# Ordered first loads on one queue, and attention features made a tile ahead, in a cosFormer attention and FFN kernel

## The chip, the cores and the metric

The kernel runs on one core of one Trainium2 chip. The metric is the device time of one execution in microseconds (us). All stage times below count from the start of the profiled span, which is about 2 us shorter than the timed execution. PE is the matrix engine (PEld its weight loads), ACT ScalarE, DVE VectorE, POOL GpSimd, SP the sync engine.

## The reference, cut to what matters

```
# q, k, v: (batch 8, heads 8, sequence 576, head_dim 64), f32
phi(x) = concat(relu(x) * cos(theta_s), relu(x) * sin(theta_s))     # 128 features
kv  = sum_s phi(k)^T v ;  z = sum_s phi(k)
x   = phi(q) kv / (phi(q) z + 1e-6)            # -> 4608 tokens x 512
out = ((x @ w1) * (x @ w2)) @ w3 @ w_out       # w1, w2: 512x1024, w3: 1024x1024, w_out: 1024x512
```

Nothing is nonlinear between w3 and w_out, so the kernel multiplies these two once at the start (its `w34b`) and then needs three products per FFN tile of 512 tokens. There are eight batches of attention and nine FFN tiles.

## The kernel before

The weights come on POOL's queue, which casts them to bf16 on the way, and the first two batches on SP's queue beside them. The features of batch 0 stand between the two halves of the weight product:

```
for i in range(4):
    nc.gpsimd.dma_start(out=w3b[:, 0:4, ts(i, 256)], in_=w3v[:, 0:4, ts(i, 256)])
    nc.gpsimd.dma_start(out=woutb[:, ts(i, 2), :], in_=wov[:, ts(i, 2), :])
    ...
for i in range(2):
    nc.gpsimd.dma_start(out=w3b[:, 4:8, ts(i, 512)], in_=w3v[:, 4:8, ts(i, 512)])
cosv, sinv = _trig_tables(nc, const)
...
load(0)                                   # k, v, q on nc.sync, six transfers
for i in range(4):                        # w1 and w2 in quarters on nc.gpsimd
    ...
load(1)                                   # on nc.sync
...
w34_half(0)
for c in range(NCH):
    prep(0, c)                            # features of batch 0
w34_half(1)
for u in attention_units(0):
    u()
```

`prep(b, c)` makes the features of one of five sequence chunks with five instructions: a relu and scale of k and of q on DVE and again on ACT, and the copy of v into `va` on POOL. Attention of a batch is twenty units: five kv products, five transposes of q features, five num steps (a PE product, then three DVE instructions that divide by the denominator), and five transposes of the result into the FFN input. All num steps share one PSUM tile, so they form a serial chain through PE and DVE.

The FFN tile t is cut into 24 groups of four matmuls each. Between the groups stand the features and then the attention units of batch t+1, both in the same tile:

```
todo = pr[0:2] + [f for p in zip(pr[2:], at[0:3]) for f in p] + at[3:]
```

For odd batches the first q transpose in that list takes chunk 4, whose features were issued last.

## Time and profile before

| | before |
|---|---|
| time, median (range) | 308.52 us (308.38 to 308.71, 4 runs) |
| profiled span | 306.4 us |
| first FFN matmul of tile 0 | 55.3 |
| first FFN matmul of tile 1 | 91.9 |
| tiles 2 to 6 | 141.7 in all |
| tiles 7, 8 and tail | 45.4 |

The page's line of PE's busy time, and the PE clock that was granted in each fortieth of the span, in tenths of full speed:

```profile
PE 265.0 (86%) x2074; PEld 141.8 (46%) x2112; DVE 160.2 (52%) x358; ACT 141.5 (46%) x249; POOL 38.0 (12%) x68
PEclk9999599796899999999999999999999999999999
```

PE is busy for 86% of the span. Of the 41 us in which it is not, 30 lie in the first third (before 91.9): there it waits, and the clock falls to 0.5 to 0.8 in some slices. About 5 of the rest are waits in tiles 2, 4 and 6. Two lines of the timeline bound the serial chain of attention of batch 0 (start, duration, engine, line, operation):

```profile
46.19 0.43 DVE L202 CAST kvs<-pnum 128x260 bf16<-128x260 f32 x1
...
55.25 0.61 PE L278 MATMUL ffnps<-xT,w1b 128*128 128x512 bf16 x1
```

From the end of the kv copy (46.6) to the first FFN matmul it takes 8.6.

### The profile page before, as it was taken

How to read it: one execution, taken by the hardware profiler on the slowest of the kernel's cores; microseconds unless marked ns; L12 is line 12 of the kernel's file. 1: busy time of each engine (PE TensorE's matmuls, PEld its weight loads, DVE VectorE, ACT ScalarE, POOL GpSimd, SP SyncE). 2: the span in 40 equal slices, each digit the busy share in tenths (PEclk: the TensorE clock that was granted, in tenths of full speed). 3: DMA queues.
4: the chain of work that ended last, by engine and by line, in shares of the span. 5: the costliest groups of instructions: out<-in, count | busy, mean ns of one | idle time of the engine just before them, and what ended most of it. 6: DMA issues, size and time to landing. Idle time of an engine off the chain costs nothing.

```text
span 306.4 us, 5315 instructions
## 1 busy us (share of the span) xinstructions
PE 265.0 (86%) x2074; PEld 141.8 (46%) x2112; DVE 160.2 (52%) x358; ACT 141.5 (46%) x249; POOL 38.0 (12%) x68
## 2 busy tenths in 40 slices
PE   0176795895989999799999998999999799999994
PEld 0133364342655554455555544555554455444441
DVE  0425248373666665666568474848746485240420
ACT  1006532274249436823862593269247524433332
POOL 8322412040000300030003002100300000000000
PEclk9999599796899999999999999999999999999999
DMA  8999999970029914981594389039812002102103
GB/s 193 246 238 224 235 238 239 300 165 2 13 92 240 257 28 137 255 186 49 174 260 122 104 225 259 19 136 260 203 71 68 2 0 91 49 0 105 34 2 135
DMA packets 51385, 43.33 MB, mean 141 GB/s; under 512 B 13985, under 2 KB 46753, under 8 KB 51361
## 3 DMA queue, kind: packets, MB, share of 16 engines
q1 hardware_dynamic: 42880, 37.75, 46.6%
q0 software_dynamic: 8480, 5.24, 11.5%
q8 instruction: 16, 0.26, 0.4%
q14 instruction: 9, 0.07, 0.1%
HBM read 38.80 MB, written 9.44 MB: 157 GB/s over the span
## 4 chain that ended last, share of the span: by engine, by line
PE 77%; ACT 9%; DVE 6%; issue 4%; DMA 3%; POOL 0%; ACTq 0%; POOLq 0%
PE ffnps L292 20%; PE ffnps L278 18%; PE ffnps L285 17%; PE ffnps L133 6%; PE pst L210 6%; ACT qp L181 4%; PE pnum L218 4%; PE pnum L196 3%; ACT kp L177 3%; DMA woutb<-in_moe_w_out_dram 3%; PE pst L244 2%; ACT asb L281 2%; DVE xblk L225 1%; PE pst L140 1%; DVE kp L175 1%
## 5 line engine op out<-in xcount | busy, mean ns | idle before, releaser
L287 DVE TENSOR_TENSOR abT<-asb,ffnps 128x512 bf16<-128x512 bf16 x72 | 49.4, 686 | 61.1 <-PE ffnps L285 56.4
L285 PE MATMUL ffnps<-xT,w2b 128*128 128x512 bf16 x285 | 75.0, 385 | 0.3 <-issue 0.2
L278 PE MATMUL ffnps<-xT,w1b 128*128 128x512 bf16 x268 | 73.2, 386 | 2.0 <-issue 0.7
L292 PE MATMUL ffnps<-w34b,abT 128*128 128x512 bf16 x275 | 69.7, 379 | 0.7
L281 ACT CAST asb<-ffnps 128x512 bf16<-128x512 f32 x72 | 41.8, 581 | 60.3 <-PE ffnps L278 60.3
L178 POOL CAST va<-vs 128x512 bf16<-128x512 f32 (+1 forms) x40 | 23.3, 626 | 164.1 <-DMA vs<-in_v_dram 138.4
L285 PEld LDWEIGHTS <-w2b 128*128 128x128 bf16 x288 | 27.3, 100 | 28.8 <-issue 2.1
L278 PEld LDWEIGHTS <-w1b 128*128 128x128 bf16 x288 | 25.4, 99 | 25.2 <-issue 1.9
L245 ACT COPY xT<-pst 128x512 bf16<-128x512 bf16 (+1 forms) x40 | 21.7, 544 | 30.4 <-PE pst L244 30.4
L297 ACT COPY osb<-ffnps 128x512 f32<-128x512 f32 x36 | 21.1, 585 | 30.6 <-PE ffnps L292 30.6
L292 PEld LDWEIGHTS <-abT 128*128 128x128 bf16 x288 | 25.0, 98 | 21.3
L211 DVE COPY qpT<-pst 128x1024 bf16<-128x1024 bf16 (+1 forms) x40 | 25.3, 632 | 14.1 <-PE pst L210 13.8
L210 PE MATMUL pst<-identb,qp 128*128 128x128 bf16 (+1 forms) x320 | 23.4, 217 | 8.8 <-ACT qp L181 8.8
L133 PE MATMUL ffnps<-woutb,w3T 128*128 128x512 bf16 x62 | 19.8, 451 | 11.2 <-DVE w3T L145 11.2
L177 ACT ACTIVATE kp<-ks,sinv 128x512 bf16<-128x512 f32 (+1 forms) x40 | 28.9, 722 | 0.0
L181 ACT ACTIVATE qp<-qs,sinv 128x512 bf16<-128x512 f32 (+1 forms) x40 | 28.5, 712 | 0.0
L225 DVE TENSOR_TENSOR xblk<-pnum,den 128x512 bf16<-128x512 f32 (+1 forms) x40 | 27.6, 689 | 1.4
L210 PEld LDWEIGHTS <-qp 128*128 128x128 bf16 (+1 forms) x320 | 18.8, 99 | 16.6 <-ACT qp L181 10.8
L218 PEld LDWEIGHTS <-qpT 128*128 128x128 bf16 (+1 forms) x320 | 14.4, 100 | 15.5 <-DVE xblk L225 6.5
L222 DVE TENSOR_SCALAR den<-pnum 128x8 f32<-128x8 f32 (+1 forms) x40 | 6.5, 163 | 28.1 <-PE pnum L218 28.1
L218 PE MATMUL pnum<-kvs,qpT 128*128 128x65 bf16 (+1 forms) x320 | 17.0, 194 | 4.0 <-DVE xblk L225 2.9
L196 PEld LDWEIGHTS <-kp 128*128 128x128 bf16 (+1 forms) x320 | 15.1, 99 | 10.5 <-issue 4.1
(40 smaller groups left out, 149.2 us busy)
## 6 DMA issues: line engine op xcount, KB each, us to landing
ks<-in_k_dram SPq DMA_DIRECT2D x8, 1024.0 KB, 7.8
vs<-in_v_dram SPq DMA_DIRECT2D x8, 1024.0 KB, 11.5
qs<-in_q_dram SPq DMA_DIRECT2D x8, 1024.0 KB, 10.7
out_dram<-osb SPq DMA_DIRECT2D x32, 256.0 KB, 2.3
ks<-in_k_dram SPq DMA_DIRECT2D x8, 128.0 KB, 8.2
w3b<-in_moe_w_dram POOLq DMA_DIRECT2D x4, 256.0 KB, 11.4
woutb<-in_moe_w_out_dram POOLq DMA_DIRECT2D x4, 256.0 KB, 12.7
vs<-in_v_dram SPq DMA_DIRECT2D x8, 128.0 KB, 11.5
```

The lines of the kernel that those rows point to most:

```text
L133: nc.tensor.matmul(acc[jp][:, :], lhsT=w3T[:, ts(jp, 128)], rhs=woutb[:, lc, :], start=(lc == 0), stop=(lc == 7))
L177: nc.scalar.activation(out=kp[:R, c, :, D:F], in_=ks, func=ACTF.Relu, scale=sc, bias=0.0)
L181: nc.scalar.activation(out=qp[:R, c, :, D:F], in_=qs, func=ACTF.Relu, scale=sc, bias=0.0)
L210: nc.tensor.transpose(pst[:, h, 0:R], qp[:R, c, h, :], identb[:R, :R])
L211: nc.vector.tensor_copy(out=att[b]["qpT"][:, :, ds(128 * c, R)], in_=pst[:, :, 0:R])
L218: nc.tensor.matmul(nt[:R, h // 4, ds((h % 4) * 65, 65)], lhsT=qpT[:, h, ds(128 * c, R)], rhs=kvs[:, h, :], start=True, stop=True)
L225: nc.vector.tensor_tensor(out=xblk[:R], in0=n4[:, :, :, 0:D], in1=den[:R].unsqueeze(3).to_broadcast([R, 2, 4, D]), op=ALU.mult)
L278: nc.tensor.matmul(aT[:, :], lhsT=w1b[:, kc, ts(jc, 128)], rhs=x[:, kc, :], start=(kc == 0), stop=(kc == 3))
L281: nc.scalar.copy(out=asb[:], in_=aT[:, :])
L285: nc.tensor.matmul(bT[:, :], lhsT=w2b[:, kc, ts(jc, 128)], rhs=x[:, kc, :], start=(kc == 0), stop=(kc == 3))
L287: nc.vector.tensor_mul(out=abT[:, jc, :], in0=asb[:], in1=bT[:, :])
L292: nc.tensor.matmul(ops[:, :], lhsT=abT[:, jc, ts(ms, 128)], rhs=w34b[:, jc, :], start=(jc == 0), stop=(jc == 7))
```

## The change

Its intent is twofold. The first loads all go on POOL in the order of their use, so that the weight product no longer shares the transfer engines with batches 0 and 1; the features of batch 0 move behind the whole weight product. And the features of batch t+2 are made in tile t, so that in tile t the attention of batch t+1 never waits for features just issued. In tile 0 this leaves features of batch 1 in the last nine groups and puts the whole attention of batch 1 behind the tile.

```diff
+    cosv, sinv = _trig_tables(nc, const)
     identb = const.tile([P, P], BF16, name="identb")
-    for i in range(4):
-        nc.gpsimd.dma_start(out=w3b[:, 0:4, ts(i, 256)], in_=w3v[:, 0:4, ts(i, 256)])
-        nc.gpsimd.dma_start(out=woutb[:, ts(i, 2), :], in_=wov[:, ts(i, 2), :])
+    for i, (c0, n) in enumerate(((0, 2), (2, 2), (4, 4))):
+        ls = slice(128 * c0, 128 * (c0 + n))
+        nc.gpsimd.dma_start(out=w3b[:, 0:4, ls], in_=w3v[:, 0:4, ls])
+        nc.gpsimd.dma_start(out=woutb[:, c0:c0 + n, :], in_=wov[:, c0:c0 + n, :])
 ...
-    load(0)
-    for i in range(4):
-        cs = ts(i, 256)
-        nc.gpsimd.dma_start(out=w1b[:, :, cs], in_=w1v[:, :, cs])
-        nc.gpsimd.dma_start(out=w2b[:, :, cs], in_=w2v[:, :, cs])
-    load(1)
+    load(0, nc.gpsimd)
+    for c0, n in ((0, 256), (256, 256), (512, 512)):
+        nc.gpsimd.dma_start(out=w1b[:, :, ds(c0, n)], in_=w1v[:, :, ds(c0, n)])
+        nc.gpsimd.dma_start(out=w2b[:, :, ds(c0, n)], in_=w2v[:, :, ds(c0, n)])
+    load(1, nc.gpsimd)
 ...   (prep is split into prep_k: k features and the v copy, and prep_q)
     w34_half(0)
-    for c in range(NCH):
-        prep(0, c)
     w34_half(1)
-    for u in attention_units(0):
+    for u in prep_units(0) + attention_units(0):
         u()
 ...
+        if t == 0:
+            spread(prep_units(1), 15, 23, slots)
+            slots[23] += prep_units(2)[0:4] + attention_units(1) + prep_units(2)[4:]
+            load(2, nc.sync)
+        else:
+            if t + 2 < B:
+                spread(prep_units(t + 2), 0, 22, slots)
+                if t + 3 < B:
+                    load(t + 3, nc.sync)
+            if t + 1 < B:
+                spread(attention_units(t + 1), 0, 22, slots)
 ...   (behind the groups of the tile)
+        if t == 0:
+            load(3, nc.sync)
```

More of the change, by code (lines that the diff above doesn't have):

```diff
@@ L98 @@
     for i in range(2):
-        nc.gpsimd.dma_start(out=w3b[:, 4:8, ts(i, 512)], in_=w3v[:, 4:8, ts(i, 512)])
-    cosv, sinv = _trig_tables(nc, const)
+        nc.gpsimd.dma_start(out=w3b[:, ds(4 + 2 * i, 2), :], in_=w3v[:, ds(4 + 2 * i, 2), :])
     va_bufs = []
@@ L108, with load @@
     raw = {}
-    def load(b):
+    def load(b, eng):
         got = []
@@ L113, in load @@
             t = ld.tile([P, H, 4, D], FP32, name=name + "s")
-            nc.sync.dma_start(out=t[:], in_=src[b, :, 0:512, :].rearrange("h (p j) d -> p h j d", j=4))
+            eng.dma_start(out=t[:], in_=src[b, :, 0:512, :].rearrange("h (p j) d -> p h j d", j=4))
             t4 = ld.tile([64, H, D], FP32, name=name + "s4")
-            nc.sync.dma_start(out=t4[:], in_=src[b, :, 512:S, :].rearrange("h p d -> p h d"))
+            eng.dma_start(out=t4[:], in_=src[b, :, 512:S, :].rearrange("h p d -> p h d"))
             got.append((t, t4))
         raw[b] = got
-    load(0)
-    for i in range(4):
-        cs = ts(i, 256)
-        nc.gpsimd.dma_start(out=w1b[:, :, cs], in_=w1v[:, :, cs])
-        nc.gpsimd.dma_start(out=w2b[:, :, cs], in_=w2v[:, :, cs])
-    load(1)
+    load(0, nc.gpsimd)
[3 more added lines that the diff above has]
+    load(1, nc.gpsimd)
     def w34_half(half):
@@ L158, with prep_k @@
     feat = {}
-    def prep(b, c):
+    def prep_k(b, c):
         R = ROWS[c]
@@ L169, in prep, with prep_q @@
         kp, qp, va = feat[b]
-        (k0, k4), (v0, v4), (q0, q4) = raw[b]
+        (k0, k4), (v0, v4), _ = raw[b]
         ks = k0[:, :, c, :] if c < 4 else k4[:]
         vs = v0[:, :, c, :] if c < 4 else v4[:]
-        qs = q0[:, :, c, :] if c < 4 else q4[:]
-        cc, sc = cosv[:R, c:c + 1], sinv[:R, c:c + 1]
-        nc.vector.tensor_scalar(out=kp[:R, c, :, 0:D], in0=ks, scalar1=0.0, scalar2=cc,
-                                op0=ALU.max, op1=ALU.mult)
-        nc.scalar.activation(out=kp[:R, c, :, D:F], in_=ks, func=ACTF.Relu, scale=sc, bias=0.0)
-        nc.gpsimd.tensor_copy(out=va[:R, c, :, 0:D], in_=vs)
-        nc.vector.tensor_scalar(out=qp[:R, c, :, 0:D], in0=qs, scalar1=0.0, scalar2=cc,
-                                op0=ALU.max, op1=ALU.mult)
-        nc.scalar.activation(out=qp[:R, c, :, D:F], in_=qs, func=ACTF.Relu, scale=sc, bias=0.0)
+        nc.vector.tensor_scalar(out=kp[:R, c, :, 0:D], in0=ks, scalar1=0.0,
+                                scalar2=cosv[:R, c:c + 1], op0=ALU.max, op1=ALU.mult)
+        nc.scalar.activation(out=kp[:R, c, :, D:F], in_=ks, func=ACTF.Relu,
+                             scale=sinv[:R, c:c + 1], bias=0.0)
+        nc.gpsimd.tensor_copy(out=va[:R, c, :, 0:D], in_=vs)
+    def prep_q(b, c):
+        R = ROWS[c]
+        qp = feat[b][1]
+        q0, q4 = raw[b][2]
+        qs = q0[:, :, c, :] if c < 4 else q4[:]
+        nc.vector.tensor_scalar(out=qp[:R, c, :, 0:D], in0=qs, scalar1=0.0,
+                                scalar2=cosv[:R, c:c + 1], op0=ALU.max, op1=ALU.mult)
+        nc.scalar.activation(out=qp[:R, c, :, D:F], in_=qs, func=ACTF.Relu,
+                             scale=sinv[:R, c:c + 1], bias=0.0)
     att = {}
@@ L300, in ffn_groups, with prep_units @@
             yield
+    def prep_units(b):
+        return ([(lambda c=c: prep_k(b, c)) for c in range(NCH)]
+                + [(lambda c=c: prep_q(b, c)) for c in range(NCH)])
     w34_half(0)
-    for c in range(NCH):
-        prep(0, c)
     w34_half(1)
@@ L308, with spread @@
     fsb = ctx.enter_context(tc.tile_pool(name="fsb", bufs=3))
-    for u in attention_units(0):
+    for u in prep_units(0) + attention_units(0):
         u()
+    def spread(units, first, last, slots):
+        for i, u in enumerate(units):
+            slots[min(last, first + int(i * (last + 1 - first) / len(units)))].append(u)
     for t in range(NT):
-        groups = ffn_groups(t)
-        n = 24
-        b = t + 1
-        todo = []
-        if b < B:
-            if b + 1 < B:
-                load(b + 1)
-            first = 8 if t == 0 else 0
-            pr = [(lambda c=c: prep(b, c)) for c in range(NCH)]
-            at = attention_units(b)
-            todo = pr[0:2] + [f for p in zip(pr[2:], at[0:3]) for f in p] + at[3:]
-            per = len(todo) / (n - first)
-        done = 0
-        for g in range(n):
-            next(groups)
-            if todo:
-                want = min(len(todo), int(round((g + 1 - first) * per)))
-                while done < want:
-                    todo[done]()
-                    done += 1
-        for _ in groups:
-            pass
-        while todo and done < len(todo):
-            todo[done]()
-            done += 1
+        slots = [[] for _ in range(24)]
+        if t == 0:
[9 more added lines that the diff above has]
+                spread(attention_units(t + 1), 0, 22, slots)
+        for g, _ in enumerate(ffn_groups(t)):
+            for u in slots[g]:
+                u()
+        if t == 0:
+            load(3, nc.sync)
 _INS = ['q', 'k', 'v', 'moe_w1', 'moe_w2', 'moe_w3', 'moe_w_out']
```

## The prediction

> **What bounds the kernel now.** I read the page by slices first, then the POOL instructions in order of time, the chain of waits by stage, and one table by stretches. Times are microseconds from the start of the span; the span is 306.4 and the timed run 308.48, so 2.1 lie outside.
>
> The slices (7.66 us each) show two stages:
>
> ```profile
> PE   0176795895989999799999998999999799999994
> DMA  8999999970029914981594389039812002102103
> GB/s 193 246 238 224 235 238 239 300 165 2 13 92 240 257 28 137 255 186 49 174 260 122 104 225 259 19 136 260 203 71 68 2 0 91 49 0 105 34 2 135
> ```
>
> For the first eight slices the transfer engines are full and PE is not. From slice 12 on PE is nearly full and the transfers have holes. So the start is set by the order in which bytes arrive, and the rest by PE. The stages in numbers, cut at the FFN tile starts in the chain that ended last:
>
> ```profile
> 0.00:56.08 56.08, 30.56 (x268) 17.72 (x271) 22.73 (x69) 17.21 (x29) 20.39 (x38) 0.93 1.18 236
> 91.89:119.33 27.44, 27.23 (x233) 14.87 (x237) 17.84 (x39) 15.42 (x28) 2.84 (x5) 1.00 0.65 168
> 119.33:148.38 29.05, 27.00 (x233) 14.91 (x238) 17.97 (x39) 15.62 (x29) 2.84 (x5) 1.00 0.63 159
> 148.38:175.60 27.22, 27.01 (x233) 14.72 (x236) 17.83 (x39) 15.84 (x29) 2.84 (x5) 1.00 0.66 170
> 175.60:204.69 29.09, 27.04 (x234) 14.96 (x238) 17.97 (x39) 15.67 (x29) 2.84 (x5) 1.00 0.61 159
> ```
>
> The second column is the length, the third the PE busy time. FFN tiles 1 and 3 take about 27.3 with 27.0 to 27.2 of PE; tiles 2 and 4 (and 6, 29.10) take 29.1 with the same PE work. The waits of PE name the difference: the first line is tile 0, the second a stretch of tiles 3 and 4.
>
> ```profile
> PE pst L210 <- ACT qp L181: 3.8, 1, 3.8
> PE pst L210 <- ACT qp L181: 1.7, 1, 1.7
> ```
>
> For an odd batch the attention takes chunk 4 first, so the transpose of its q feature stands right behind the ten feature instructions that ScalarE still works off. It occurs in tiles 0, 2, 4 and 6, whose next batch is odd.
>
> The POOL instructions show how the start is queued:
>
> ```profile
> 7.01 0.73 POOL L95 DMA_DIRECT2D woutb<-in_moe_w_out_dram  x1
> 8.40 0.77 POOL L99 DMA_DIRECT2D w3b<-in_moe_w_dram  x1 [0.65 <-DMA w3b<-in_moe_w_dram]
> 10.43 0.74 POOL L99 DMA_DIRECT2D w3b<-in_moe_w_dram  x1 [1.26 <-DMA woutb<-in_moe_w_out_dram]
> 13.58 0.76 POOL L123 DMA_DIRECT2D w1b<-in_moe_w_dram  x1 [1.78 <-DMA w3b<-in_moe_w_dram]
> 32.87 0.74 POOL L124 DMA_DIRECT2D w2b<-in_moe_w_dram  x1 [3.46 <-DMA w3b<-in_moe_w_dram]
> 33.60 2.83 POOL L178 CAST va<-vs 128x512 bf16<-128x512 f32 x5
> ```
>
> Eight transfers go out at once; the ninth waits for a w3b landing at 8.4, the tenth for a woutb, the eleventh for a w3b, and so on to the eighteenth. I read this as: **transfer n on this queue is issued when transfer n-8 has landed**. The copies of v for batch 0 stand behind the eighteenth. Today that costs nothing, because attention of batch 0 begins only at 43.1.
>
> **What the Trainium skill says.** "DMA: Bandwidth & Descriptors", section "Queues, rings and completion order": each transfer engine takes turns between the queues that have work, packet by packet. The trace agrees: the last eight weight pieces (4096 packets) land between 32.9 and 56.7 while the loads of q, k, v move 3.5 MB. The same page, "Issuing engines are not separate DMA queues": issuing from several engines only saves issue time. Here too the total stays near 236 GB/s with two queues, so one ordered queue loses nothing by itself; no stretch of this trace has the weight queue alone. "PSUM — Partial Sum Buffer", "Engine vs sequencer instructions": the queues of ScalarE, VectorE and GpSimd are strict FIFO. The va copies behind the last issue at 32.87 agree. "TensorE: Matmul & The Clock Gate", Part 1: an idle window halves the PE clock, some 3.4 us of work restore it. The trace agrees in kind: four 128x512 matmuls take 0.86 in the chain when warm, so eight take 1.73; after attention of batch 0, in which PE is idle for half of the time, the first eight of tile 0 take from 55.32 to 58.58, or 3.26. I charge 1.5 for such a start.
>
> **The change part by part.** *(a) Order of loads.* All 26 first transfers go on POOL: w3 and w_out (8), load of batch 0 (6), w1 and w2 (6), load of batch 1 (6). Rates: a load alone moves 260 GB/s (150 to 164), so 3.54 MB take 13.7. The weights are 10.5 MB at the source: taking 13.7 for the loads out of the 23.8 that w1 and w2 (4.2 MB) took beside them leaves 10.1, or 25 for all; their queue's share (11.5% of 306.4) gives 35. I choose 30, or 1.5 per half MB. From a first byte at 2.6 the stream then passes: first four pieces 8.6, all w_out and half of w3 14.6, all w3 20.6, batch 0 34.3, the first halves of w1 and w2 40.3. A landing comes about 2 later. So w3 is complete at 22.6 instead of 32.9, and the second half of the w3*w_out product, which took 14.4 from 28.4 with a 3.4 wait for VectorE and a cold clock, ends near 34 instead of 42.85. **Gain for PE so far: 9.**
>
> *(b) What takes it back.* The v copies of batch 0 now stand behind transfer 26, which waits for transfer 18, the second quarter of w2. Features of k for batch 0 run from 34 to 37 (5 x 0.62 on ScalarE), free their raw buffer, and the load of batch 2 on SP begins to share the engines. By 37 some 1.8 of the four quarter pieces are through; the remaining 2.2 cost 3.0 each when shared (23.8 / 8), so data at 43.6, landing 45.6. Transfer 26 is issued by 46.4, five copies take 2.8: 49.2. Then the last kv product, the kv copies (0.9), and the serial chain of five num steps, which today takes 8.6 from the end of the kv copy (46.6) to the first FFN matmul (55.25). **FFN tile 0 starts at 59.2, 4.0 later than now.** Without (b) it would be near 48.
>
> *(c) Tile 0.* Nothing but features of batch 1 is mixed in, in the last nine slots: 20.7 (as tile 7: 261.0 to 281.7) plus 1.5 cold clock gives 81.4. Attention of batch 1 now stands whole behind the tile. ScalarE is about 1 behind by then and first makes four more k features (2.5), so the kv copy ends 4.3 after the tile, plus 8.6: 12.9. Tile 1 starts at 94.3, against 91.89 now. So the tile-0 stage is 35.1 against 36.6: the 3.8 wait and the cold matmuls behind it go, but about 13 of attention of which only some 6.25 is PE work is laid bare. Tile 1 then begins cold (1.5) and with six features ahead of its evacuations (0.5 after four PSUM buffers of slack).
>
> *(d) Tiles 1 to 6.* Features are made a whole tile ahead, so the 1.7 waits in tiles 2, 4 and 6 go. Six tiles at 27.2 are 163.2, against 169.1 now: **gain 5.9**. Per tile ScalarE has some 16 and VectorE 18 of 27, so neither becomes the bound. The matmuls, features and copies are the same in number.
>
> *(e) Tiles 7 and 8 and the tail.* Untouched: 45.4.
>
> Sum: 94.3 + 2.0 + 163.2 + 45.4 = 304.9, plus 2.1 = 307.0.
>
> **The rivals.** *First: the v copies do not hold attention of batch 0 up*, because the order on POOL or the eight-transfer limit is not as I read it. Then FFN tile 0 starts at 48 and the time is 296. For it: the change is plainly built to start FFN early. Against it: 33.60 follows 32.87 on POOL without a gap. *Second: one software queue is slower alone than beside another.* For it: the transfer share exceeds 1 only with two queues (1.18 to 1.27 against 1.04 for a load alone). With 25% longer transfers transfer 18 lands near 51 and the time is 312 to 313. *Third: the bare attention after tile 0 costs less* since VectorE has no FFN work then; at best 2 off, 305. *Fourth: the steady tiles gain nothing*, because a wait for kv or for the late load of batch 3 replaces the removed one; then 312. Against it: that load is issued near 82 and takes 14, while its q features come in the middle of tile 1.
>
> **Range and chances.** The middle of the argument is 305 to 309; the second rival stretches it up, the first down. I give 302 to 313. Faster by over 2% needs 302.3 or less: the first rival (10%) and a part of good luck in transfers, 17% together. Slower needs 314.7: slow transfers and lost steady gain at once, 7%. Within 2%: 76%.
>
> **What would show it.** The w3 pieces should all have landed near 23 and the second product end near 34; POOL should wait for weight landings until about 46 and make the v copies only then, with PE waiting for them; the first FFN matmul at about 59; tile 1 near 94 after a stretch of about 13 with PE half idle; tiles 1 to 6 equal at about 27.2 with no wait of the q transposes for ScalarE. The prediction is wrong if the v copies come before 40, if the w3 pieces land after 28, or if tiles 2, 4 and 6 stay above 28.5.

## The result

The changed kernel takes 305.12 us in the median (304.74 to 305.78, four runs), against 308.52. A run is called slow when it is over 1.5% above the fastest of the same kernel; slow runs are left out of the ratios. The ratio is 0.9892 with a 95% interval of 0.9871 to 0.9912. A ratio here is the mean time of one kernel's fast runs over that of the other's of the same rounds, so it is not quite the ratio of the medians. The gain of 1.1% is clear of noise; 0.5% was forecast.

The page after, in the order of the lines shown of before: PE's busy time, its busy share by slices, its clock, and the transfers (slices of 7.57 us).

```profile
PE 268.1 (89%) x2112; PEld 145.0 (48%) x2112; DVE 160.6 (53%) x358; ACT 143.2 (47%) x249; POOL 45.8 (15%) x76
PE   1979027899877999999999999999999999999994
PEclk9999757599979999999999999999999999999999
DMA  7999999990499943791397269320013002103103
```

PE now starts early (slices 1 to 3), then has a hole: in slice 4 (30 to 38 us) it is idle. A second thin place lies in slices 11 and 12, around 84 to 98 us. From slice 13 on it is full. The transfers are full over the first nine slices nearly as before, and the page's GB/s rows add up to 15.9 MB over the first ten slices in both: the same bytes move in the same time, in another order. The table of stretches (limits, length, PE busy; the two numbers ahead of the last are the granted clock and the transfer share):

```profile
57.70:79.60 21.90, 21.90 (x97) 9.62 (x96) 11.04 (x22) 11.52 (x21) 5.70 (x10) 0.93 0.57 137
79.60:93.60 14.00, 9.16 (x144) 7.29 (x143) 8.91 (x23) 6.66 (x13) 0.93 (x2) 0.88 0.93 246
93.60:121.11 27.51, 27.36 (x238) 14.95 (x236) 21.14 (x45) 19.36 (x34) 5.73 (x9) 1.00 0.71 180
121.11:148.28 27.17, 27.17 (x237) 14.89 (x236) 17.58 (x39) 16.02 (x28) 3.04 (x5) 1.00 0.64 169
148.28:175.47 27.19, 27.19 (x238) 14.90 (x236) 17.68 (x39) 16.02 (x28) 3.04 (x5) 1.00 0.64 171
```

Tile 0 is 21.9 long, the bare attention of batch 1 takes 14.0, and tiles 2 and 3 are equal at 27.2 with PE busy throughout. Before, they were 29.1 and 27.2. The waits of PE up to the first FFN matmul, longest first:

```profile
PE pnum L203 <- POOL va L177: 13.5, 1, 13.5
PE pst L140 <- DMA w3b<-in_moe_w_dram: 6.4, 2, 5.6
```

One wait of 13.5 us for the v copies of batch 0 is the hole. After 121 us the same view lists no wait of PE at all. What POOL did ahead of the copies:

```profile
30.95 0.83 POOL L124 DMA_DIRECT2D w2b<-in_moe_w_dram  x1 [0.23 <-DMA vs<-in_v_dram]
...
37.08 0.69 POOL L117 DMA_DIRECT2D vs<-in_v_dram  x1
39.05 0.89 POOL L115 DMA_DIRECT2D qs<-in_q_dram  x1 [1.28 <-DMA w1b<-in_moe_w_dram]
42.17 0.69 POOL L117 DMA_DIRECT2D qs<-in_q_dram  x1 [2.24 <-DMA w2b<-in_moe_w_dram]
42.86 2.85 POOL L177 CAST va<-vs 128x512 bf16<-128x512 f32 x5
```

The v data of batch 0 had landed before 30.95, for an issue that waited for it goes out there. The copies came 12 us later, because POOL first had to issue the six transfers of batch 1, the last of which waited for a landing of w2.

The stages side by side, cut where the chain that ended last enters each tile. A stage is the difference of two such starts.

| stage | before | predicted | after |
|---|---|---|---|
| to the first FFN matmul of tile 0 | 55.3 | 59.2 | 57.7 |
| tile 0 and attention of batch 1 | 36.6 | 35.1 | 35.7 |
| tile 1 | 27.4 | 29.2 | 27.7 |
| tiles 2 to 6 | 141.7 | 136.0 | 135.9 |
| tiles 7, 8 and tail | 45.4 | 45.4 | 45.6 |
| span | 306.4 | 304.9 | 302.6 |

So 5.8 us come from tiles 2 to 6 and 0.9 from tile 0, while the start loses 2.4.

### The profile page after: what moved, and what is told of

The parts are those of the page before. It is cut to its first block, busy times and chain, and to the rows that moved or that the text cites. A ratio compares the mean times of both kernels' runs of the same rounds, so it can differ in the third digit from the quotient of the medians.

```text
span 302.6 us, 5330 instructions
## 1 busy us (share of the span) xinstructions
PE 268.1 (89%) x2112; PEld 145.0 (48%) x2112; DVE 160.6 (53%) x358; ACT 143.2 (47%) x249; POOL 45.8 (15%) x76
## 3 DMA queue, kind: packets, MB, share of 16 engines
q1 hardware_dynamic: 33472, 30.68, 37.7%
## 4 chain that ended last, share of the span: by engine, by line
PE 77%; DMA 11%; ACT 4%; DVE 3%; POOL 3%; issue 1%; POOLq 0%; ACTq 0%
PE ffnps L292 21%; PE ffnps L299 21%; PE ffnps L285 20%; DMA w2b<-in_moe_w_dram 5%; DMA ks<-in_k_dram 5%; PE pst L217 5%; PE pnum L225 4%; PE pnum L203 3%; PE pst L251 3%; DVE xblk L232 2%; ACT qp L187 1%; ACT kp L175 1%; POOL woutb L97 1%; POOL w3b L96 1%; DVE den L230 0%
## 5 line engine op out<-in xcount | busy, mean ns | idle before, releaser
L294 DVE TENSOR_TENSOR abT<-asb,ffnps 128x512 bf16<-128x512 bf16 x72 | 49.3, 685 | 71.8 <-PE ffnps L292 68.7
L285 PE MATMUL ffnps<-xT,w1b 128*128 128x512 bf16 x288 | 74.7, 382 | 0.1
L177 POOL CAST va<-vs 128x512 bf16<-128x512 f32 (+1 forms) x40 | 24.3, 652 | 125.0 <-DMA vs<-in_v_dram 66.2
L299 PEld LDWEIGHTS <-abT 128*128 128x128 bf16 x288 | 26.2, 98 | 25.8
L292 PEld LDWEIGHTS <-w2b 128*128 128x128 bf16 x288 | 25.1, 98 | 24.3 <-issue 1.1
L304 ACT COPY osb<-ffnps 128x512 f32<-128x512 f32 x36 | 21.1, 586 | 22.6 <-PE ffnps L299 16.1
L203 PE MATMUL pnum<-va,kp 128*128 128x65 bf16 (+1 forms) x320 | 17.2, 198 | 13.5 <-POOL va L177 13.5
L175 ACT ACTIVATE kp<-ks,sinv 128x512 bf16<-128x512 f32 (+1 forms) x40 | 27.8, 720 | 0.0
L217 PE MATMUL pst<-identb,qp 128*128 128x128 bf16 (+1 forms) x320 | 25.0, 225 | 0.9 <-ACT qp L187 0.8
L217 PEld LDWEIGHTS <-qp 128*128 128x128 bf16 (+1 forms) x320 | 20.7, 103 | 9.4 <-issue 1.3
L225 PE MATMUL pnum<-kvs,qpT 128*128 128x65 bf16 (+1 forms) x320 | 18.0, 200 | 5.4 <-DVE xblk L232 3.1
L185 DVE TENSOR_SCALAR qp<-qs,cosv 128x512 bf16<-128x512 f32 (+1 forms) x40 | 21.0, 548 | 1.2 <-DMA qs<-in_q_dram 1.2
```

What stands on the lines that cost most here:

```text
L175: nc.scalar.activation(out=kp[:R, c, :, D:F], in_=ks, func=ACTF.Relu, scale=sinv[:R, c:c + 1], bias=0.0)
L203: nc.tensor.matmul(kvt[:, h // 4, ds((h % 4) * 65, 65)], lhsT=kp[:R, c, h, :], rhs=va[:R, c, h, :], start=(c == 0 and h % 4 == 0), stop=(c ...
L217: nc.tensor.transpose(pst[:, h, 0:R], qp[:R, c, h, :], identb[:R, :R])
L225: nc.tensor.matmul(nt[:R, h // 4, ds((h % 4) * 65, 65)], lhsT=qpT[:, h, ds(128 * c, R)], rhs=kvs[:, h, :], start=True, stop=True)
L285: nc.tensor.matmul(aT[:, :], lhsT=w1b[:, kc, ts(jc, 128)], rhs=x[:, kc, :], start=(kc == 0), stop=(kc == 3))
L292: nc.tensor.matmul(bT[:, :], lhsT=w2b[:, kc, ts(jc, 128)], rhs=x[:, kc, :], start=(kc == 0), stop=(kc == 3))
```

## The experiments

My theory after the result: the part that makes features ahead gives the gain; the part that orders the loads gains 9 us or more for the weight product and loses it again, because the v copies of batch 0 stand in POOL's order behind the issue of batch 1's loads. The rival: the order of loads is itself what helps, and attention of batch 0 is held by something else. All runs gave correct results, and each is compared with the kernel before on the same chip. The experiments ran on three chips, on which the kernel before took 308.2 to 308.5 in the median (310.1 in the short repeat e7_again); where two changed kernels are compared, compare their ratios.

### e1_v_copies_first

```diff
-    load(1, nc.gpsimd)          # ahead of the weight product
 ...
-    for u in prep_units(0) + attention_units(0):
+    for u in prep_units(0):
+        u()
+    load(1, nc.gpsimd)          # behind the v copies of batch 0
+    for u in attention_units(0):
         u()
```

> The changed kernel with one edit: the six transfers of batch 1 are issued on POOL behind the v copies of batch 0, not ahead of them. Theory (the copies wait in POOL's order for transfer 26, which waits for the landing of transfer 18): v of batch 0 landed before 31, so the copies come at 31 to 34 instead of 42.9; PE no longer waits 13.5 us for them; the q features (ScalarE until 37) then release the kv copy, and the serial chain of 9.2 us puts the first FFN matmul at 46 to 48 instead of 57.7. If all of it is kept, the time is 294 to 296. Rival A (attention of batch 0 is held by something else, so POOL's order is not the cause): first FFN matmul stays at 56 to 58, time 304 to 306. Rival B (the start moves, but the loads of batches 1 and 2 now land too late for the features in the last slots of tile 0, so the gain is given back): first FFN matmul at 47 but the end of tile 0 is stretched by a wait for q of batch 1, time 298 to 303.

Measured: 299.32 us (296.67 to 300.97), ratio to before 0.9679 (0.9602 to 0.9755). From POOL's timeline and from the chain that ended last:

```profile
31.38 3.70 POOL L176 CAST va<-vs 128x512 bf16<-128x512 f32 x5
35.03 0.91 POOL L115 DMA_DIRECT2D ks<-in_k_dram  x1
...
30.90 3.71 DVE kp L172 x5
```

The copies come at 31.4 as expected, the first FFN matmul at 49.3 instead of 57.7. Rival A falls: moving this one thing moves the start by 8.4. The start is still 1 to 3 later than expected. The last line shows a part of it: the five k features on DVE take 3.71 while the copies run on POOL, against 2.18 in the changed kernel, where they do not run together. The time is 3 to 5 above the expected 294 to 296, but not for Rival B's reason: PE has no wait for q of batch 1 beyond the 0.8 that the changed kernel has too. The trace is of the execution with the lowest clock of the four (300.29 us at 0.941; the fastest had 296.67 at 0.959). In it the stage of tile 0 and its attention is 37.4 long at a mean clock of 0.82, and tile 1 is 29.8 instead of 27.7 at 0.91; the filler runs below take up the clock again.

### e2_q_behind

The same, but only the two q transfers of batch 1 go behind the copies: `load(1, nc.gpsimd, "kv")` stays, and `load(1, nc.gpsimd, "q")` follows `prep_units(0)`.

> The changed kernel with only the two q transfers of batch 1 issued behind the v copies of batch 0. Theory (transfer n waits for the landing of transfer n-8): the last transfer ahead of the copies is now number 24, whose partner 16 is the first quarter of w2; in the changed kernel transfer 24 was issued at 37.1 without a wait, so the copies come at 37.8 instead of 42.9, a step of about 5 between the changed kernel and the run with all six behind; first FFN matmul near 52.5, time about 300. Rival A: no movement, 304 to 306. Rival C (the copies wait for the v data or for the whole queue to drain, not for a count of eight): the copies come either where the run with all six behind has them or stay at 42.9, not in between.

Measured: 299.21 us in the median, of which one execution of four is slow (303.64); fast ones 298.48 to 299.29, ratio 0.9688 (0.9642 to 0.9735).

```profile
PE pnum L204 <- POOL va L178: 7.5, 1, 7.5
...
36.76 2.84 POOL L178 CAST va<-vs 128x512 bf16<-128x512 f32 x5
```

The copies stand at 36.8, between 31.4 and 42.9, and PE's wait is 7.5 instead of 13.5. The first FFN matmul comes at 52.2 (expected 52.5). That is the step that a count of eight transfers in flight asks for, and Rival C falls with Rival A. In time it is no worse than the run with all six behind, though its start is 3 us later: its DVE features of batch 0 (30.5 to 35.4) and its POOL copies do not meet, and its stages after the start are 35.7 and 27.5.

### p1_order_only and p2_features_only

Each takes one part of the change alone. The first is the kernel before with the new load block on POOL, the table constants first and `prep(0, c)` moved behind `w34_half(1)`. The second is the changed kernel with the old load block and `prep` of batch 0 between the halves again.

> The kernel before with the order part of the change alone: all first loads on POOL in the order of use, table constants first, features of batch 0 behind both halves of the weight product; features and attention of batch 1 on as before. Theory: the start is that of the changed kernel, first FFN matmul near 57.7 against 55.25, and tile 0 and the later tiles keep their waits for ScalarE (3.8 and 1.7): 2.5 slower than before, 310 to 312. Rival (the order of loads is what makes the changed kernel faster): 303 to 306.

> The features-ahead part of the change alone, with the loads and the start of the kernel before. Theory: first FFN matmul at 55.25 as before, tile 0 about 22 long, bare attention of batch 1 about 14, tiles 1 to 6 at 27.2 to 27.7, no wait of PE for the q features: 302 to 304, that is faster than the changed kernel by 2 to 3. Rival (the two parts need each other, since loads of batch 1 and 2 come late without the ordered queue): 306 to 309.

Measured: the order alone 307.63 us, ratio 0.9986 (0.9933 to 1.0040). The features alone 305.92 us, ratio 0.9914 (0.9875 to 0.9952). PE's waits of the first, from 40 us on:

```profile
PE pnum L196 <- POOL va L178: 11.3, 1, 11.3
PE pst L210 <- ACT qp L181: 8.9, 4, 3.8
```

The order alone wins nothing: the hole is there (11.3), and so are the four waits for ScalarE in tiles 0, 2, 4 and 6 that the other part removes. I had expected it to lose 2 to 3 us. Its copies came at 40.8 rather than 42.9, its first FFN matmul at 55.7, so it lost nothing either. Transfer 18 landed at 39.9 instead of 41.9, and SP's load of batch 2 began at 37.7 instead of 33.2; that fits the prediction's step that this load shares the transfer engines, but no run tests it. The features alone reach 0.9914, which the interval of the whole change (0.9871 to 0.9912) all but touches: within the noise the gain of the change is that of this part, and the order of loads adds nothing clear to it. I had expected 302 to 304. Its start came at 57.0 instead of 55.3 and its next two stages were 37.3 and 28.5, against 35.7 and 27.7 in the changed kernel. From 43 us to the first FFN matmul the granted clock was 0.72, against 0.98 in the kernel before with the same loads, and the chain from the kv copy took 9.4 instead of 8.6. Why the clock was lower stays open. The two stages (the granted clock is the third number from the end):

```profile
57.02:94.33 37.31, 32.25 (x237) 17.55 (x238) 20.05 (x45) 18.17 (x32) 2.99 (x6) 0.87 0.70 169
94.33:122.82 28.49, 28.06 (x234) 15.40 (x238) 21.73 (x45) 19.47 (x34) 6.41 (x10) 0.95 0.72 175
```

### e3_attn1_mixed

```diff
-            spread(prep_units(1), 15, 23, slots)
-            slots[23] += prep_units(2)[0:4] + attention_units(1) + prep_units(2)[4:]
+            spread(prep_units(1)[0:5], 3, 7, slots)
+            spread([prep_units(1)[5 + c] for c in (4, 0, 1, 2, 3)], 8, 12, slots)
+            spread(prep_units(2)[0:5], 16, 23, slots)
+            spread(attention_units(1), 10, 23, slots)
 ...   (tile 1: q features of batch 2 in slots 0-6, attention 2 in 3-23, features of batch 3 in 8-22)
```

> The changed kernel with the attention of batch 1 spread over the slots of tile 0 (features of k of batch 1 in slots 3 to 7, of q in 8 to 12, attention in 10 to 23, k features of batch 2 in 16 to 23, its q features at the start of tile 1). Theory (bare attention of batch 1 costs its 14 us minus its own PE work of 6.3 to 6.5): the stage from the first FFN matmul of tile 0 (57.7) to that of tile 1 (93.4 in the changed kernel, 35.7) shrinks to 28 to 30, so 6 to 7 less; the loads of batch 1 have landed by about 65, which is slot 8. Time 298 to 300. Rival (nothing is won, because ScalarE becomes the bound of tile 0, with 16 features beside its evacuations, and PE waits for it): stage of 33 or more, time 303 to 306.

Measured: 301.43 us (300.72 to 302.49), ratio 0.9762 (0.9725 to 0.9799). The stage from the first FFN matmul of tile 0 to that of tile 1 went from 35.7 to 30.1 (58.2 to 88.3). So the bare attention did cost 5 to 6 us, nearly what was expected. Some of it comes back at the start of tile 2, which is 28.9 long: PE waits 1.7 us for a ScalarE evacuation. That evacuation had itself stood still for 4.8 us, until an output transfer freed its buffer. The transfer in the chain that ended last:

```profile
115.15 5.31 DMA out_dram<-osb
```

The median of these transfers is 2.3 us. What made it slow was not tested.

### e4_scalar_order

```diff
-            slots[23] += prep_units(2)[0:4] + attention_units(1) + prep_units(2)[4:]
+            pr, at = prep_units(2), attention_units(1)
+            slots[23] += at[0:7]
+            for i, u in enumerate(at[7:]):
+                slots[23].append(u)
+                if i < len(pr):
+                    slots[23].append(pr[i])
```

> The changed kernel with the ten features of batch 2 moved: none ahead of the attention of batch 1, each behind one of its later steps, where ScalarE is idle. Theory (four k features of 2.45 us on ScalarE stand ahead of the kv copy on the path): the kv copy comes 2.5 earlier, the stage after tile 0 is 11.4 instead of 13.9, and the six features ahead of the first evacuations of tile 1 are gone too: 302 to 303, with a VectorE feature of 0.4 now and then inside the serial chain, which may give back up to 1.5. Rival (the serial chain on VectorE is lengthened by as much as is won): 304.5 to 306.

Measured: 310.47 us (308.52 to 311.06), ratio 1.0041 (0.9994 to 1.0087). It is 5 us worse than the changed kernel, worse even than the rival had it. The chain that ended last in the changed kernel, and then in this one:

```profile
81.41 2.45 ACT kp L175 x4
83.86 0.27 ACT kvs L208
```

```profile
84.99 0.37 PE pnum L203 x8
...
90.66 0.60 DVE qpT L218
91.25 0.79 DVE kp L173 x2
92.04 0.09 DVE den L229
```

I had read the four ScalarE features in the first chain as a cost of 2.45. But the chain shows only which of two waits ended last. With them gone the kv copy waits for PE's last kv product instead, and comes 3.7 after the tile's end instead of 4.2. What I put into the serial chain, however, counts nearly in full: 4.3 us of DVE features stand in it, and from the kv copy to tile 1 it takes 12.5 instead of 8.9. Tile 1's first matmuls then take some 0.5 us each instead of 0.26. Of the two places, the changed kernel's is the better one; e3 has a third. Not all of the 6.3 us between the two spans is the edit's: tile 0 started at 58.7 instead of 57.7 and took 22.9 instead of 21.9, before any moved feature. The traces of the changed kernel, e3 and e4, which share all the code up to there, start tile 0 at 57.7, 58.2 and 58.7, so a single trace tells a start to about 1 us.

### e5_both and e6_both_ordered

Both have the edit of e1 and a mix as in e3, with the slots moved to where batch 1 has landed (in e5 the k features in 7 to 11, q in 12 to 16, attention in 14 to 23). e6 also puts batch 2 on the ordered queue and begins some three slots earlier (4, 9 and 11):

```diff
     load(1, nc.gpsimd)
+    load(2, nc.gpsimd)
 ...
-            load(2, nc.sync)
```

> Both repairs together: the v copies of batch 0 ahead of the loads of batch 1 in POOL's order, and the attention of batch 1 spread over slots 14 to 23 of tile 0 (k features in 7 to 11, q features in 12 to 16). Theory: first FFN matmul at 49, tile 0 about 29 to 31, tile 1 at 78 to 80 and then 27.2 a tile: span 287 to 290, time 289 to 292. Rival (the loads of batch 1 land at 58 to 66 whatever stands in tile 0, so the in-order engines stall in their features and PE behind them): time 295 to 299, no better than the first repair alone.

> As the run with both repairs, with the load of batch 2 put on the same POOL queue behind that of batch 1, so that it no longer shares the transfer engines with w1, w2 and batch 1, and the features and attention of batch 1 begin some three slots earlier. Theory (the sharing is what makes batch 1 land at 58 to 66): v of batch 1 lands near 54 and q near 59 instead; the time is 288 to 291 with fewer waits in tile 0. Rival (one queue moves fewer bytes than two: 1.04 to 1.10 busy share alone against 1.2 to 1.3 shared): batch 1 lands no earlier and batch 2 near 75, and the time is that of the other run or 1 to 2 worse.

Measured: e5 293.29 us (293.07 to 294.42), ratio 0.9507 (0.9467 to 0.9547); e6 291.81 us (291.39 to 292.12), ratio 0.9447 (0.9416 to 0.9477). Tile 0 starts at 48.4 and 49.7, tile 1 at 80.3 and 79.9. Together the repairs save more than they do one by one: against the changed kernel the ratio falls by 0.021 in e1, by 0.013 in e3 and by 0.039 in e5. Both times are some 1 us above what I expected, but the rivals fall: e5 is well below e1 (0.9507 against 0.9679), and every execution of e6 is faster than every one of e5. The v copies of batch 1 in e6 begin at 53.7 (e5: 57.8), so the ordered load does land earlier; the tiles' starts differ by little, since in e6 the start is 1.3 later. A likely reason stands in DVE's timeline (in e5 the same five features take 3.58) and in the view of its line (durations in ns: lowest, median, highest):

```profile
30.33 5.57 DVE L172 TENSOR_SCALAR kp<-ks,cosv 128x512 bf16<-128x512 f32 x5
...
L172 DVE TENSOR_SCALAR kp<-ks,cosv x40: 466/477/3496, 30.3 to 202.1; 128x512 bf16<-128x512 f32 x32, 64x512 bf16<-64x512 f32 x8
```

One feature of 0.48 took 3.50 while POOL made its five copies from 31.1 to 33.9. The Trainium skill, "SBUF — State Buffer", section "Who interferes with whom", says that DVE in its two-port modes and GpSimd lock a shared port pair, and that the one that issues second is blocked until the other finishes; the trace agrees in kind.

### e7_warm_clock, e7_again and e8_best_warm

The filler is a matmul whose result nobody reads; it removes nothing and only keeps PE busy:

```diff
+    def fill(n):
+        f = ps_ffn.tile([P, 512], FP32, name="ffnps")
+        for _ in range(n):
+            nc.tensor.matmul(f[:, :], lhsT=w34b[:, 0, 0:128], rhs=w34b[:, 0, :], start=True, stop=True)
 ...
+    fill(54)                                   # e8: 16
+    for i, u in enumerate(attention_units(0)):
         u()
+        if i in (8, 11, 14, 16, 18):
+            fill(3)
```

> The changed kernel with matmuls whose result nobody reads, put on PE while it waits: 54 ahead of the attention of batch 0 (where PE waits 13.5 us for the v copies) and three behind each of its five num steps. Nothing on the path is removed; only PE is kept busy. Theory (the granted clock of PE falls while it waits, and the attention of batch 0 and the first FFN matmuls then run at half speed, which my sum left out for the one and charged for the other): from the first v copy to the first FFN matmul 12.4 to 13 instead of 14.9, and the first eight FFN matmuls of tile 0 in 1.7 instead of 3.4; together 3 to 4 off, 301 to 302.5. Rival (the serial chain of VectorE sets the length whatever PE's clock, and the filler only delays the num products): 304.5 to 307.

> The same kernel as the filler run on the changed kernel, once more, because that run's trace fell in the slow state (307.3) while its three other executions were at 300.1 to 300.7. Theory: in a fast execution the eight first FFN matmuls of tile 0 take 1.7 to 1.9 and the first ones of tile 1 also run at full clock; FFN tile 0 starts near 55.5 and tile 1 near 89.5 to 91, against 57.7 and 93.4 in the changed kernel; 300 to 301. Rival: the gain of the filler run lies in the later tiles, which would then be shorter than 27.2 each, and the starts are unchanged.

> The run with both repairs and batch 2 on the ordered queue, with the same filler matmuls (16 ahead of the attention of batch 0, three behind each num step). Theory: the first eight FFN matmuls of tile 0 and the kv products run at full clock, 2 to 3 off: 289 to 290. Rival (filler stands in front of useful products, as PE waits only short times here): 291.5 to 293.

Measured on the changed kernel: three fast executions at 300.06 to 300.67, ratio 0.9724 (0.9679 to 0.9769), and one slow at 307.3; the repeat had one fast at 300.93 and one slow at 305.56. Both traces fell on a slow execution, so I have no trace of a fast one and do not explain the slow ones. What the records of the fast executions show is the mean granted clock: 0.988 to 1.000, against 0.941 to 0.955 in the four of the changed kernel without filler. So filler alone, with every instruction of the path in place, is worth 4 to 5 us there; where exactly it falls, and so whether my expectation for the starts held, stays open.

On the best version the filler gives 288.65 us (288.50 to 290.53), ratio 0.9368 (0.9315 to 0.9421), at a clock of 0.994 to 1.000, and here both traces are of fast executions. The chain at the start of tile 0, first without and then with filler:

```profile
49.80 0.54 PE ffnps L284
50.34 0.22 issue
50.56 1.06 PE ffnps L284 x2
51.62 1.71 PE ffnps L291 x4
```

```profile
47.46 0.97 PE ffnps L284 x4
48.43 0.86 PE ffnps L291 x4
```

The first eight FFN matmuls take 3.53 without and 1.83 with it, and the chain from the kv copy to them 9.2 and 8.6. So the clock accounts for about 2.3 us here (1.7 and 0.6), of the 3.2 by which the medians differ. The features on DVE were also shorter in this trace (five in 3.63 instead of 5.49) and the kv copy ended 1.7 earlier, which has nothing to do with the filler's purpose; the later stages give some of it back.

## Why the prediction was wrong

Its mechanism was right in the main; three terms of its sum were mis-sized. Half a MB of weights on the ordered queue was charged 1.5 us and took 1.26; the way from the first v copy to the first FFN matmul was charged 12.8 and took 14.9; the cold start of tile 1 was charged 2.0 and cost 0.5. The first two have opposite signs, so that the start came out as near as it did partly by luck. A gain of 1.5 us was forecast and 3.4 measured. By its own steps:

- **(a) The order of loads: right, with the transfer term too large.** I took 1.5 us per half MB of weights. In the trace POOL's issues that wait for w_out and w3 pieces of 1 MB follow each other at 13.40, 15.92, 18.40 and 20.98, so 1.25 to 1.3 per half MB. All of w3 had landed near 20.7 (predicted 22.6, of which 2 for a landing rest on no line shown), the product ended at 30.7 (34), and transfer 18 landed near 41.9 (45.6). The choice of the middle between 25 and 35 us for all weights was the error; the additive reading, 25, was the better one.
- **(b) The v copies hold attention of batch 0: right.** They came at 42.9 behind transfer 26 (46.4 predicted), PE waited 13.5 for them, and e1 and e2 move both by the edits that the reading of eight in flight asks for. The step after it was too small: from the first copy to the first FFN matmul I had 12.8, and it took 14.9. I charged a cold clock to the FFN matmuls but not to the kv products and q transposes ahead of them, which follow a 13.5 us wait: sixteen kv products take 1.15 there and 0.68 before, and the granted clock from the first copy to the first FFN matmul was 0.61, against 0.98 in that place before. Together the two errors leave the start 1.5 early.
- **(c) Tile 0 and its bare attention: right in kind, 0.6 too short in all.** Tile 0 took 21.9 (22.2) and the attention 13.9 (12.9), again with part of its PE work at a reduced clock (0.88 in the mean). e3 shows that 5 to 6 of the 14 can be won by mixing it in.
- **The 2.0 charged to the start of tile 1: the other mis-sized term.** PE came into tile 1 at full clock in this trace (1.00 in the table of stretches), and the six features ahead of the evacuations cost a gap of under 0.2 at 98 us. The tile took 27.7, not 29.2. In e1 and e4 the same place was cold, and the tile took 29.8 and 28.6, so the term is real, but I counted as certain what some traces have and others not.
- **(d) Tiles 1 to 6: right.** Tiles 2 to 6 took 135.9 (136.0), each 27.2, with no wait of PE.

The differences add up: 1.5 at the start and 1.5 in tile 1 better, 0.6 in tile 0 worse, 0.2 in the tail worse: 2.3 less than the predicted span (0.1 is rounding).

The rivals: the first, that the copies hold nothing up, fell. The second, that one software queue is slower alone, fell the other way: the queue was faster alone than I had assumed. The third and fourth fell; the bare attention cost more, not less, and nothing replaced the removed waits.

## What to carry to other kernels

An instruction that issues a transfer waits in its engine's order like any other, so compute on the same engine behind it waits for whatever the queue's limit waits for; look at what stands behind the last issue before moving loads to an engine that also computes. In a chain of waits the item named is only the latest of several, and removing it is worth no more than the distance to the next one (0.5 of 2.45 us in e4), while nearly all that was added to the serial chain counted (3.6 of 4.3). A long wait of PE can cost more than its length: after the 13.5 us wait the clock was 0.61 up to the first FFN matmul, and sixteen kv products took 1.15 instead of 0.68.

## What the Trainium skill lacked or had wrong

- "SBUF — State Buffer", "Who interferes with whom": it says the second to issue is blocked until the first finishes. Here one DVE feature was blocked across several POOL copies in a row: 3.50 us instead of 0.48, with five copies of 0.57 each running from 31.1 to 33.9. The record of that feature begins at 30.7, ahead of the copies, while POOL was issuing a transfer. The page does not say that a lock can pass from one POOL instruction to the next past a waiting DVE instruction; that this happened here is my reading of the times.
- "DMA: Bandwidth & Descriptors", "Measured (HBM→SBUF, 128 partitions, SWDGE, issued from GpSimd)" under Bandwidth: the table has 341 GB/s for a transfer of 1 MB (the 6.15 us of the same row would be 170). Queued one behind the other, 1 MB pieces that are cast from f32 to bf16 landed every 2.5 us, which is 415 GB/s at the source. The page gives no figure for casting transfers queued one behind the other.
- No page that I read has the limit of eight transfers in flight on POOL's queue as this kernel is built. Transfer 26 waited for transfer 18; with two fewer ahead of them the v copies came 6.1 us earlier, with six fewer 11.5 us earlier.
- "TensorE: Matmul & The Clock Gate", Part 1, puts the ramp penalty at under 1% of a typical kernel span. Here the clock fell again after waits (0.61 from the v copies to the first FFN matmul, 0.88 in the bare attention), and filler took 4 to 5 us of 305 off, some 1.5%.
